# Sigmoid attention with a mixture of experts on one core: the half slots' first layer multiplies the high weights with high and low tokens in one product

## The chip, the core and the metric

The kernel runs on one core of a Trainium2 chip. TensorE (PE) multiplies matrices and leaves the sums in eight banks of PSUM, each 128 partitions by 512 fp32 columns. VectorE (DVE), ScalarE (ACT) and GpSimd (POOL) do the rest, each one instruction at a time in the order of the program. SyncE (SP) starts most DMAs. The metric is device time of one execution in microseconds.

## The reference

Attention runs on 8 batches of 12 heads, 448 tokens and 64 dimensions, with a sigmoid in place of the softmax. Its output, seen as 3584 tokens of 768 numbers, goes through 8 experts, of which each token uses one:

```
attn = 1 / (1 + exp(-(scale * q @ k.T - log(S))));  x = (attn @ v) as 3584 x 768
e_idx = argmax(x @ w_gate, 1)
gate_w = softmax(x @ w_gate)[e_idx];  eom = sigmoid(x @ w_output_gate)
for e in range(8):
    h = maximum(x[e_idx == e] @ w1[e], 0)          # 768 -> 1024
    out[e_idx == e] = gate_w * eom[:, e] * (h @ w2[e])   # 1024 -> 768
```

All data are fp32.

## The kernel before

The first half of the span computes attention and the lists of tokens of each expert. Then come the experts, in slots of one expert each. A full slot takes TB = 448 tokens, a half slot TM = 240. In the profiled execution seven full slots and two half slots run (the diff touches the half slots alone); up to six more half slots stand in the program and are skipped by a branch.

Every fp32 operand is split into a high part, rounded to a format that TensorE takes at full rate, and a low part, the remainder. A product is the sum of three: high by high, high by low, low by high. ACT makes the high part (L414, a cast) and DVE the low part (L415, a subtraction).

**Layer 1 of a half slot** makes eight blocks f = 0 to 7 of 128 hidden features. A block sums over six pieces d of the 768 inputs, three products each: wh·xh (L467), wh·xl (L468), wl·xh (L469), each 240 columns, all into one PSUM bank. Three banks (`psh`) rotate, so block f + 3 may start only when the last reader of block f is done. The readers are the relu on ACT (L496, writes the high part hh) and one DVE instruction (L497, max(ps, 0) − hh, the low part hl). In the loop over f (L589), behind blocks 1 to 4, `split_w2(f - 1)` splits two rows of the second layer's weights: two casts on ACT, two subtractions of 768 columns on DVE. Behind blocks 2 to 4 SP is given the next slot's w1 loads (L400), which overwrite the raw w2 rows just split.

**Layer 1 of a full slot** already joins wh·xh and wh·xl: `xs` lies as 448 high and 448 low columns side by side, so products of 512, 384 and 448 columns do it, and the 64 columns that lie in the wrong place are copied to SBUF and added back by DVE (`join`, L485 and L486) ahead of the relu.

**Layer 2 of a half slot** has four pieces of 24 products of 384 columns (L527 to L529), each evicted on ACT (L534). Around them ACT and DVE split the next slot's w1 and tokens.

**Pending blocks.** A full slot leaves the last two of its six output blocks in PSUM. The next slot's `finish` (L539) turns them: per block `join`, then a DVE transpose (L517), then eight DMAs to DRAM, four loads back, scaling on ACT (L564) and scatters on POOL. `slot` calls `next(fin)` for the turning at L587, ahead of layer 1, in both kinds of slot.

The instructions of each engine stand in the order in which the program gives them (`manual_schedule`). Between the full slots and the first half slot lies the end of nested branches (L932), where each engine also waits for its own DMAs.

Of the kernel before, what the change touches and what calls it, by code (L numbers as in the profile page):

```python
# [8 lines left out]
F32 = mybir.dt.float32  # L9
# [4 lines left out]
ALU = mybir.AluOpType  # L14
# [8 lines left out]
DM = H * D  # L23
DF = 1024
# [4 lines left out]
Q4 = DM // 4  # L29
G = 2  # L30
TB = 448
TM = 240
GB_, GM = TB // 32, -(-TM // 32)
# [19 lines left out]
def r32(ap):  # L53
    return ap.bitcast(F32)


class Kernel:
# [19 lines left out]
    def memory(self):  # L77
        self.rounded = self.pool("rounded").tile([128, ROUNDED // 4], F32R, name="rounded")
        self.plain = self.pool("plain").tile([128, PLAIN // 4], F32, name="plain")
        ps = self.pool("psum", space=PSUM).tile([128, 8, 512], F32, name="ps")  # L80
        self.ps_s = [ps[:, 0:2], ps[:, 2:4]]
        self.ps_o = [[ps[:, 4], ps[:, 5]], [ps[:, 6], ps[:, 7]]]
        self.ps_s2 = ps[:, 6:8]
        self.psh = [ps[:, i] for i in (0, 1, 2)]
        self.psy = [ps[:, i] for i in (4, 5, 3)]
        self.ps_step = ps[:, 3, 0:8]
        self.rot = {}
        self.beat = [None, None]
        self.hints = {2: [ET.Activation, ET.DVE, ET.Pool]}

        c = self.carve
        w = c(0, 3, 2, 2, DF)
        self.w1s = [[w[:, d // 2, a, d % 2] for d in range(6)] for a in range(2)]
        self.w1p = [[w[:, k, a] for k in range(3)] for a in range(2)]
        self.x2 = c(12 * DF * 4, 6, 2 * TB)
        self.xs = [self.x2[:, :, TB * i:TB * i + TB] for i in range(2)]
        self.slots_begun = 0

        self.w1r = c(0, 6, DF, dt=F32)
        self.w2r = c(0, 8, DM, dt=F32)  # L100
        self.xg = c(6 * DF * 4, GB_, Q4, dt=F32)
        self.xT = c(6 * DF * 4 + XG, 6, TB, dt=F32)
        self.yq = c(6 * DF * 4 + XG, GB_, Q4, dt=F32)
        self.xTm = c(6 * DF * 4 + XG, 6, 32 * GM, dt=F32)
        self.spare = c(6 * DF * 4 + GM * Q4 * 4, DM, dt=F32), c(6 * DF * 4 + XG + 6 * 32 * GM * 4, DM, dt=F32)

    def late_memory(self):
# [350 lines left out]
    def layer1_mm(self, f, n):  # L458
        nc = self.nc
        ps = self.h_ps = self.take("h", self.psh)  # L460
        c = slice(128 * f, 128 * f + 128)
        (wh, wl), (xh, xl) = self.w1s, self.xs
        for d in range(6):
            if n == TB and self.joined:
                mm = self.products(ps, wh[d][:, c], wl[d][:, c], self.x2[:, d], d == 0, d == 5)
            else:
                nc.tensor.matmul(ps[:, 0:n], wh[d][:, c], xh[:, d, 0:n], start=(d == 0), stop=False)  # L467
                nc.tensor.matmul(ps[:, 0:n], wh[d][:, c], xl[:, d, 0:n], start=False, stop=False)  # L468
                mm = nc.tensor.matmul(ps[:, 0:n], wl[d][:, c], xh[:, d, 0:n], start=False, stop=(d == 5))  # L469
            if d == 2:  # L470
                self.beat[1] = mm.ins
# [16 lines left out]
    def layer1(self, f, n, begun=False):  # L488
        nc = self.nc
        if not begun:  # L490
            self.layer1_mm(f, n)
        if n == TB and self.joined:
            self.join(self.h_ps)
        ps = self.h_ps[:, 0:n]
        hh, hl = (h[:, f, 0:n] for h in self.hs)
        self.beat[0] = nc.scalar.activation(hh, ps, AF.Relu).ins  # L496
        nc.vector.scalar_tensor_tensor(hl, ps, 0.0, r32(hh), ALU.max, ALU.subtract)  # L497

# [80 lines left out]
    def slot(self, cur, nxt, side=None, begun=False, hint=None):  # L579
        nx = None  # L580
        if nxt is not None:
            nx, rows, sure = nxt() if callable(nxt) else nxt
            last = -(-nx["lx"].shape[1] // 2) - 1
        n = 32 * cur["lx"].shape[1]
        lag = 0 if self.left is not None or n == TB else 2
        fin = self.finish(n)
        next(fin, None)  # L587
        self.rot["y"] = 1
        for f in range(8):  # L589
            if begun and f == 1:  # L590
                self.change_step()
            self.layer1(f, TB if n == TB else TM, begun and f == 0)
            if nx is not None and n < TB:
                if f >= lag:
                    self.gather_rows(nx, f - lag, rows, 1)
                if f == 7 and lag == 0:
                    self.nc.gpsimd.drain()
            elif nx is not None and f <= last:
                self.gather_rows(nx, 2 * f, rows, 1)
                self.gather_rows(nx, 2 * f + 1, rows, 0)  # L600
                if f == last and not sure:
                    self.nc.gpsimd.drain()
            if f == 6 and n < TB:
                next(fin, None)
            if side is not None:
                next(side, None)
            if 1 <= f < 5:
                self.split_w2(f - 1)
                if f > 1:
                    self.load_w1(nx, f - 2)  # L610
        if lag == 0:
            for k in range(3):
                self.turn_x(nx, k)
        if n == TB:
            next(fin, None)
            self.layer2_columns(cur, nx, side, hint, fin)
            self.slots_begun += 1
            return nx
        ws = {0: (0, 1), 1: (2,)}
        for i in range(4):  # L620
            t = i // 2
            self.layer2(cur, t, i % 2, self.ys[t])
            if nx is not None:
                if lag and i == 0:
                    for g in range(8 - lag, 8):
                        self.gather_rows(nx, g, rows, g % 2)
                    self.nc.gpsimd.drain()  # L627
                for k in ws.get(i, ()):
                    self.split_w1(k)
                    for j in range(k, 4 if k == 2 else k + 1):  # L630
                        self.load_w2(nx, j)
                if lag and i == 0:
                    for k in range(3):
                        self.turn_x(nx, k)
                if i < 3:
                    self.split_x(nx, i)
            if i < 2:
                next(fin, None)
            if side is not None:
                next(side, None)  # L640
            if hint is not None and i == 1:
                self.tc.mark_branch_hint_location(hint, hint="LikelyTaken", engines=[ET.SP])
        return nx
# [342 lines left out]
```

## Time and profile before

| what | value |
|---|---|
| three runs, median | 750.63 us (749.03 to 752.99) |
| profiled execution | 749.12 us, its span 747.3 us |
| PE busy | 739.1 us, 99% of the span |
| DVE, ACT, POOL busy | 447.2, 369.8, 250.4 us |
| first half slot, layer 1 | 674.93 to 691.13 us |
| second half slot, layer 1 | 707.78 to 723.91 us |

A timeline row gives the start and the duration in us, the engine, the line, the operation with what it writes and reads, and in brackets how long the engine was idle before it and what ended that. Products on PE overlap: a row's duration is longer than the distance from one start to the next, and the distance is what one product costs. The names `plain` and `rounded` are two large buffers in which many smaller ones are carved out.

### The profile page before, as it was taken

How to read it: one execution, taken by the hardware profiler on the slowest of the kernel's cores; microseconds unless marked ns; L12 is line 12 of the kernel's file. 1: busy time of each engine (PE TensorE's matmuls, PEld its weight loads, DVE VectorE, ACT ScalarE, POOL GpSimd, SP SyncE). 2: the span in 40 equal slices, each digit the busy share in tenths (PEclk: the TensorE clock that was granted, in tenths of full speed). 3: DMA queues.
4: the chain of work that ended last, by engine and by line, in shares of the span. 5: the costliest groups of instructions: out<-in, count | busy, mean ns of one | idle time of the engine just before them, and what ended most of it. 6: DMA issues, size and time to landing. Idle time of an engine off the chain costs nothing. (4 is left out here: it accounts for less than half of the span.)

```text
span 747.3 us, 14681 instructions
## 1 busy us (share of the span) xinstructions
PE 739.1 (99%) x5576; PEld 544.7 (73%) x5576; DVE 447.2 (60%) x895; ACT 369.8 (49%) x437; POOL 250.4 (34%) x375
## 2 busy tenths in 40 slices
PE   9999999999999999999999999999999999999996
PEld 4334444444344469999999999999999999999996
DVE  1333863585777849916746746646655655656555
ACT  5666676566777734404514514514514423434644
POOL 5000130022254435246525315325224234234351
PEclk9999999999999999999999999999999999999999
DMA  8464656647495755366386386386386485576951
GB/s 283 149 206 144 193 140 195 188 122 212 172 331 184 208 135 180 132 167 199 113 297 216 131 265 221 118 277 205 147 274 183 177 272 174 188 227 202 328 200 46
DMA packets 90647, 145.76 MB, mean 195 GB/s; under 512 B 16738, under 2 KB 67298, under 8 KB 90560
## 3 DMA queue, kind: packets, MB, share of 16 engines
q1 hardware_dynamic: 79808, 119.22, 51.6%
q0 software_dynamic: 9680, 24.53, 9.3%
q10 hardware_dynamic: 1072, 0.92, 0.5%
q8 instruction: 46, 0.75, 0.4%
q14 instruction: 41, 0.34, 0.1%
HBM read 118.40 MB, written 32.62 MB: 202 GB/s over the span
## 5 line engine op out<-in xcount | busy, mean ns | idle before, releaser
L718 ACT ACTIVATE a<-ps,small 128x896 f32<-128x896 f32 x168 | 168.6, 1007 | 85.6 <-PE ps L716 83.3
L716 PE MATMUL ps<-q,k 64*64 64x448 f32 x1344 | 157.6, 542 | 0.0
L389 POOL DMA_INDIRECT plain<-x_dram,lxs x112 | 111.0, 991 | 134.1 <-ACT h L496 63.4
L725 PE MATMUL ps<-a,v 64*64 64x448 f32 x1344 | 155.9, 536 | 0.0
L496 ACT ACTIVATE h<-ps 128x448 fp32r<-128x448 f32 (+1 forms) x72 | 36.4, 506 | 204.8 <-DVE ps L486 132.2
L479 PE MATMUL ps<-rounded 128*128 128x512 f32 x288 | 112.0, 389 | 0.0
L479 PE MATMUL ps<-h,w2h 128*128 128x512 f32 x288 | 112.0, 389 | 0.0
L716 PEld LDWEIGHTS ps<-q,k 64*64 64x64 f32 x1344 | 50.5, 134 | 76.5 <-issue 69.8
L725 PEld LDWEIGHTS ps<-a,v 64*64 64x64 f32 x1344 | 51.0, 133 | 75.4 <-issue 71.4
L481 PE MATMUL ps<-rounded 128*128 128x448 f32 x288 | 105.1, 365 | 0.0
L481 PE MATMUL ps<-h,w2l 128*128 128x448 f32 x288 | 105.1, 365 | 0.0
L415 DVE TENSOR_TENSOR rounded<-plain,rounded 128x2048 fp32r<-128x2048 f32 (+5 forms) x63 | 96.4, 1566 | 10.8 <-ACT rounded L414 10.8
L480 PE MATMUL ps<-rounded 128*128 128x384 f32 x288 | 95.9, 333 | 0.0
L480 PE MATMUL ps<-h,w2h 128*128 128x384 f32 x288 | 95.9, 333 | 0.0
L414 ACT CAST rounded<-plain 128x2048 fp32r<-128x2048 f32 (+5 forms) x63 | 82.0, 1332 | 24.0 <-DVE plain L434 22.8
L571 POOL DMA_INDIRECT out<-y,lts x24 | 42.9, 1786 | 106.3 <-ACT y L564 103.3
L485 DVE COPY hb<-ps 128x64 f32<-128x64 f32 x84 | 18.5, 220 | 94.8 <-PE ps L481 76.6
L415 DVE TENSOR_TENSOR w2l<-plain,w2h 128x768 fp32r<-128x768 f32 x72 | 65.7, 954 | 4.4 <-ACT w2h L414 1.9
L497 DVE SCALAR_TENSOR_TENSOR h<-ps,h 128x448 fp32r<-128x448 f32 (+1 forms) x72 | 41.1, 574 | 40.0 <-ACT h L496 35.1
L481 PEld LDWEIGHTS ps<-rounded 128*128 128x128 f32 x288 | 54.1, 188 | 11.1
L481 PEld LDWEIGHTS ps<-h,w2l 128*128 128x128 f32 x288 | 54.1, 188 | 11.1
L254 POOL TENSOR_TENSOR meta<-eom,den 64x1 f32<-64x1 f32 (+1 forms) x40 | 8.0, 199 | 152.2 <-DVE eom L251 150.5
(170 smaller groups left out, 1058.7 us busy)
## 6 DMA issues: line engine op xcount, KB each, us to landing
plain<-w SPq DMA_DIRECT2D x40, 768.0 KB
plain<-w SPq DMA_DIRECT2D x27, 1024.0 KB
k<-kT SPq DMA_DIRECT2D x23, 448.0 KB
q<-qT SPq DMA_DIRECT2D x23, 448.0 KB
x_dram<-xt SPq DMA_DIRECT2D x30, 336.0 KB
v<-vm SPq DMA_DIRECT2D x23, 384.0 KB
y<-y_dram SPq DMA_DIRECT2D x18, 384.0 KB
y_dram<-plain SPq DMA_DIRECT2D x28, 192.0 KB
```

The lines of the kernel that those rows point to most:

```text
L389: self.paced(self.nc.gpsimd.indirect_dma_start(out=self.xg[:, g], out_offset=None, in_=x4, in_offset=bass.IndirectOffsetOnAxis(ap=s["lx"][ ...
L414: self.nc.scalar.copy(hi, raw)
L415: self.nc.vector.tensor_tensor(lo, raw, r32(hi), ALU.subtract)
L479: mm(ps, wh, both[:, 0:512], start=first, stop=False)
L480: mm(ps[:, 512 - TB:TB], wh, both[:, 512:2 * TB], start=False, stop=False)
L481: return mm(ps[:, 0:TB], wl, both[:, 0:TB], start=False, stop=last)
L496: self.beat[0] = nc.scalar.activation(hh, ps, AF.Relu).ins
L497: nc.vector.scalar_tensor_tensor(hl, ps, 0.0, r32(hh), ALU.max, ALU.subtract)
L571: i = self.nc.gpsimd.indirect_dma_start(out=self.out, out_offset=bass.IndirectOffsetOnAxis(ap=at, axis=0), in_=y, in_offset=None, bounds_c ...
L716: qk = nc.tensor.matmul(ps[half[h], j, 0:S], k[half[j], e, o:o + 64], q[half[j], e], start=True, stop=True)
L718: self.beat[0] = nc.scalar.activation(at[u % 3], ps[:, :, 0:S], AF.Sigmoid, bias=self.bias_s, scale=1.0 / math.sqrt(D)).ins
L725: nc.tensor.matmul(self.ps_o[e][h][half[j], 0:S], v[half[h], e, c, j], a[half[h], j], start=(i in ((0, 3 if h else 4)[e],)), stop=(i == (2 ...
```

## The change

For half slots the products wh·xh and wh·xl become one product of 480 columns: high tokens give columns 0 to 239, low tokens columns 240 to 479 of the bank. wl·xh is added to columns 0 to 239 as before. ACT then copies columns 240 to 479 to a new SBUF buffer `rest_m`, and DVE adds them onto columns 0 to 239, ahead of the relu. In half slots the turning of the pending blocks moves from ahead of block 0 to behind it. `rest_m` lies in `plain`, in a place that holds other data in full slots. Full slots are unchanged.

```
+        self.rest_m = c(6 * DF * 4 + (GM * Q4 + DM) * 4, TM, dt=F32)
...
         for d in range(6):
-            if n == TB and self.joined:
+            if n == TM:
+                both = self.x2[:, d].rearrange("p (a t) -> p a t", a=2)[:, :, 0:n]
+                nc.tensor.matmul(ps[:, 0:2 * n].rearrange("p (a t) -> p a t", a=2), wh[d][:, c], both,
+                                 start=(d == 0), stop=False)
+                mm = nc.tensor.matmul(ps[:, 0:n], wl[d][:, c], xh[:, d, 0:n], start=False, stop=(d == 5))
+            elif self.joined:
                 mm = self.products(ps, wh[d][:, c], wl[d][:, c], self.x2[:, d], d == 0, d == 5)
...
-        if n == TB and self.joined:
-            self.join(self.h_ps)
         ps = self.h_ps[:, 0:n]
         hh, hl = (h[:, f, 0:n] for h in self.hs)
+        if n == TM:
+            nc.scalar.copy(self.rest_m, self.h_ps[:, TM:2 * TM])
+            nc.vector.tensor_tensor(ps, ps, self.rest_m, ALU.add)
+        elif self.joined:
+            self.join(self.h_ps)
         self.beat[0] = nc.scalar.activation(hh, ps, AF.Relu).ins
...
         fin = self.finish(n)
-        next(fin, None)
+        if n == TB:
+            next(fin, None)
...
             self.layer1(f, TB if n == TB else TM, begun and f == 0)
+            if f == 0 and n < TB:
+                next(fin, None)
```

In the changed kernel the copy is L501, the add L502, the relu L505, the low part L506, the cast L415, the subtraction L416, the join L491 and L492, the transpose L526.

On DVE, at the start of the first half slot, stood before (w2l is the low part of w2, h the hidden features, hb the buffer of the join):

```order
L485 COPY hb<-ps 128x64
L486 TENSOR_TENSOR ps<-ps,hb 128x64
L517 STREAM_TRANSPOSE plain<-ps 128x14x32
L485 COPY hb<-ps 128x64
L486 TENSOR_TENSOR ps<-ps,hb 128x64
L517 STREAM_TRANSPOSE plain<-ps 128x14x32
L497 SCALAR_TENSOR_TENSOR h<-ps,h 128x240 x2
L415 TENSOR_TENSOR w2l_2640<-plain,w2h_2638 128x4x6x32 x2
L497 SCALAR_TENSOR_TENSOR h<-ps,h 128x240
L415 TENSOR_TENSOR w2l_2640<-plain,w2h_2638 128x4x6x32 x2
```

The same place in the changed kernel:

```order
L502 TENSOR_TENSOR ps<-ps,plain 128x240
L506 SCALAR_TENSOR_TENSOR h<-ps,h 128x240
L491 COPY hb<-ps 128x64
L492 TENSOR_TENSOR ps<-ps,hb 128x64
L526 STREAM_TRANSPOSE plain<-ps 128x14x32
L491 COPY hb<-ps 128x64
L492 TENSOR_TENSOR ps<-ps,hb 128x64
L526 STREAM_TRANSPOSE plain<-ps 128x14x32
L502 TENSOR_TENSOR ps<-ps,plain 128x240
L506 SCALAR_TENSOR_TENSOR h<-ps,h 128x240
L416 TENSOR_TENSOR w2l_2640<-plain,w2h_2638 128x4x6x32 x2
L502 TENSOR_TENSOR ps<-ps,plain 128x240
```

The two turnings now stand between block 0 and block 1, and an add stands ahead of every low part, behind the two subtractions of the block before.

On ACT, at the same place, stood before (w2h is the high part of w2):

```order
L496 ACTIVATE h<-ps 128x240 x2
L414 CAST w2h_2638<-plain 128x4x6x32 x2
L496 ACTIVATE h<-ps 128x240
L414 CAST w2h_2638<-plain 128x4x6x32 x2
L496 ACTIVATE h<-ps 128x240
```

The same place in the changed kernel:

```order
L501 COPY plain<-ps 128x240
L505 ACTIVATE h<-ps 128x240
L501 COPY plain<-ps 128x240
L505 ACTIVATE h<-ps 128x240
L415 CAST w2h_2638<-plain 128x4x6x32 x2
L501 COPY plain<-ps 128x240
L505 ACTIVATE h<-ps 128x240
```

Each relu now stands behind a copy on its own engine, and between the two lies the add on DVE; the casts of `split_w2` stay behind the relu.

## Rows read from the trace of the kernel before

**Rows 1.** The page, part 1: busy time, share and instructions of each engine.

```profile
PE 739.1 (99%) x5576; PEld 544.7 (73%) x5576; DVE 447.2 (60%) x895; ACT 369.8 (49%) x437; POOL 250.4 (34%) x375
```

**Rows 2.** Stretches: length, busy of PE, PEld, DVE, ACT, POOL, granted clock, DMA.

```profile
674.00:691.09 17.09, 16.53 (x146) 16.22 (x146) 11.59 (x21) 8.30 (x15) 8.89 (x8) 1.00 0.63 185
740.50:747.30 6.80, 0.22 (x2) 0.00 (x0) 1.90 (x3) 0.58 (x1) 0.96 (x1) 0.75 0.18 53
```

**Rows 3.** Timeline, PE: first products of both layers in both half slots.

```profile
674.93 0.35 PE L467 MATMUL ps<-rounded 128*128 128x240 f32 x1 [0.56 <-DVE hb L485]
...
691.13 0.34 PE L527 MATMUL ps<-w2h,h 128*128 128x384 f32 x1
...
707.78 0.27 PE L467 MATMUL ps<-rounded 128*128 128x240 f32 x1
...
723.91 0.34 PE L527 MATMUL ps<-w2h,h 128*128 128x384 f32 x1
```

**Rows 4.** Timeline, PE: four products of a full slot's layer 1.

```profile
628.01 0.39 PE L479 MATMUL ps<-rounded 128*128 128x512 f32 x1
628.24 0.33 PE L480 MATMUL ps<-rounded 128*128 128x384 f32 x1
628.41 0.36 PE L481 MATMUL ps<-rounded 128*128 128x448 f32 x1
628.61 0.39 PE L479 MATMUL ps<-rounded 128*128 128x512 f32 x1
```

**Rows 5.** Timeline, DVE: one block of a full slot's layer 1.

```profile
631.26 0.22 DVE L485 COPY hb<-ps 128x64 f32<-128x64 f32 x1
631.51 0.23 DVE L486 TENSOR_TENSOR ps<-ps,hb 128x64 f32<-128x64 f32 x1
632.42 0.62 DVE L497 SCALAR_TENSOR_TENSOR h<-ps,h 128x448 fp32r<-128x448 f32 x1 [0.68 <-ACT h L496]
633.14 1.83 DVE L415 TENSOR_TENSOR w2l<-plain,w2h 128x768 fp32r<-128x768 f32 x2
634.88 0.22 DVE L485 COPY hb<-ps 128x64 f32<-128x64 f32 x1
```

**Rows 6.** Timeline, ACT: the same block.

```profile
631.84 0.55 ACT L496 ACTIVATE h<-ps 128x448 fp32r<-128x448 f32 x1 [1.62 <-DVE ps L486]
632.28 1.55 ACT L414 CAST w2h<-plain 128x768 fp32r<-128x768 f32 x2
```

**Rows 7.** Timeline, ACT: first half slot, layer 1.

```profile
677.27 0.37 ACT L496 ACTIVATE h<-ps 128x240 fp32r<-128x240 f32 x1 [8.64 <-PE ps L469]
...
682.09 0.37 ACT L496 ACTIVATE h<-ps 128x240 fp32r<-128x240 f32 x1 [0.90 <-ACT w2h L414]
682.36 1.56 ACT L414 CAST w2h<-plain 128x768 fp32r<-128x768 f32 x2
```

**Rows 8.** Timeline, DVE: first half slot, turning and layer 1.

```profile
678.16 0.65 DVE L517 STREAM_TRANSPOSE plain<-ps 128x448 f32<-128x448 f32 x1 [3.16 <-SPq L932]
...
679.79 0.68 DVE L497 SCALAR_TENSOR_TENSOR h<-ps,h 128x240 fp32r<-128x240 f32 x2
...
683.22 1.83 DVE L415 TENSOR_TENSOR w2l<-plain,w2h 128x768 fp32r<-128x768 f32 x2 [0.31 <-ACT w2h L414]
684.96 0.40 DVE L497 SCALAR_TENSOR_TENSOR h<-ps,h 128x240 fp32r<-128x240 f32 x1
```

**Rows 9.** Line 932, POOL's queue: count, least/median/most ns, first and last start.

```profile
L932 POOLq INC_SWDGE_SEM  x1: 280/280/280, 676.9 to 676.9; - x1
```

**Rows 10.** Timeline, SP, ACT and DVE: first half slot, next slot's weights and tokens.

```profile
685.38 4.17 SPq L400 DMA_DIRECT2D plain<-w  x3
...
695.63 0.58 ACT L534 ACTIVATE y<-ps,ltb 128x384 f32<-128x384 f32 x1 [3.86 <-PE ps L529]
...
708.37 0.69 DVE L415 TENSOR_TENSOR rounded<-plain,rounded 128x512 fp32r<-128x512 f32 x1 [0.23 <-ACT rounded L414]
```

**Rows 11.** Timeline, ACT: second half slot, last casts of w2.

```profile
720.25 1.57 ACT L414 CAST w2h<-plain 128x768 fp32r<-128x768 f32 x2 [1.42 <-DMA plain<-w]
```

## The prediction, as it was put on record

> **What bounds the kernel now.** I read the page's busy shares first: PE is busy 99% of the span, the others at most 60% [rows 1]. So whatever shortens PE's stream shortens the kernel, and whatever makes PE wait lengthens it. The stretch table then shows the first half slot's layer 1 with PE at 16.53 of 17.09 us, the missing 0.56 us being the pause at the end of the nested branches, and granted clock 1.00, the level of 2.4 GHz [rows 2]. PE's timeline gives the block: 144 products of 240 columns from 674.93 to 691.13, 112.5 ns each, 2.02 us per block; the second half slot needs 16.13 us for the same, so PE never waits there [rows 3]. Last I read DVE and ACT, since they hold the PSUM banks that PE needs back. They are nearly full in the blocks with weight splits: DVE's two subtractions take 1.74 us (683.22 to 684.96) and the low part 0.3 to 0.4 beside PE's 2.02 [rows 8].
>
> **What PE gains.** Each d loses one product and gets a wider one. In a full slot 512, 384 and 448 columns cost 0.23, 0.17 and 0.20 us from start to start [rows 4], so 480 columns, halfway between 448 and 512, cost 0.215. Before: 3 x 0.1125 = 0.3375 per d. After: 0.215 + 0.1125 = 0.3275. That is 0.01 x 48 = 0.5 us per half slot, 1.0 us in all, and a block of 1.96 us. No row shows moving columns taken from two pieces. The bounds are the two measured widths around it: at 0.20 the gain is 0.025 x 96 = 2.4 us, at 0.23 it is a loss of 0.005 x 96 = 0.5. I take the middle between them.
>
> The Trainium skill, "TensorE: Matmul & The Clock Gate", section "Back-to-back issue gap", gives a warm product columns / 2.4 GHz plus about 2.5 ns: 102.5 ns for 240 columns. The rows have 112.5, so by it a dropped product saves 2.5 ns, 0.24 us over 96, in place of 1.0. The measurement decides, and the forecast below hardly uses either.
>
> **What the change adds on ACT and DVE.** Per block a copy of 240 columns out of PSUM on ACT (priced as the relu of that width, 0.37 us [rows 7]) and an add of 240 columns on DVE. The add with 64 columns starts 0.33 us ahead of the relu that waits for it (631.51 to 631.84) [rows 5, 6]. The low part costs 0.62 us at 448 columns and 0.40 at 240 [rows 5, 8], so 176 more columns are about 0.19, and add to relu is 0.52 us. Bounds for it: 0.33 (width free) and 0.95 + 0.1 (a subtraction of 768 columns).
>
> Alone these are small. What matters is that they tie two queues into a ring. Before, ACT's relu and DVE's low part waited for PE and each other's last result only, and the casts ran ahead of the subtractions. Now block f + 1's relu waits for its add, the add stands in DVE's queue behind the two subtractions of block f, these wait for the casts, and the casts stand in ACT's queue behind block f's relu. One turn of the ring: add to relu 0.52; relu to cast 0.27 (682.09 to 682.36); first cast to first subtraction 0.86 (682.36 to 683.22); the two subtractions to the next instruction 1.74 (683.22 to 684.96) [rows 7, 8]. Sum 3.39 us, against PE's 1.96. The full slots already run this ring: 631.26 to 634.88 is 3.62 us, and its parts, 0.25 + 0.33 + 0.44 + 0.86 + 1.74, make 3.62 [rows 5, 6]. There it hides since a block takes PE 3.6 us (6 x 0.60 [rows 4]); a half slot's block takes half of that.
>
> **First half slot.** Block 0 leaves PE at 674.93 + 1.96 = 676.89. Before, the relu came 0.32 behind the block's end (677.27 against 676.95); so the copy starts at 677.21. The copy waits newly for POOL's queues, whose counter is set at 676.9 + 0.28 = 677.18 [rows 9]: just in time, and I add 0.04. Behind ACT stand only the relu and casts, which wait anyway. Copy end and handover 0.41: add at 677.66, relu 678.18, low part 678.59, DVE free at 678.90. Now come the two turnings: the first join 0.51, then 1.63 as before from the first transpose to the low part (678.16 to 679.79) [rows 8], so add 1 starts at 681.04. The 3.16 us that DVE waited for SP ahead of its first transpose is covered now by block 0 [rows 8], which gains little: that wait ran beside PE's block 0. Behind the moved turnings SP's eight DMAs to DRAM start some 1.2 us later.
>
> Adds 2, 3, 4 follow every 3.39: 684.43, 687.82, 691.21. A low part ends 0.52 + 0.41 + 0.40 = 1.33 behind its add's start, and PE may go on about 0.15 later. Block 7 needs the bank of block 4: 691.21 + 1.33 + 0.15 = 692.69. It ends at 694.65, where layer 2 began at 691.13: **3.5 us later**. PE should stand before blocks 5, 6 and 7 for 1.2, 1.4 and 1.4 us, less the 0.5 it gains. Blocks 5 to 7 are not followed by splits; their ring is 1.6 us and layer 2, which reads h in the order of f, meets them in time.
>
> What follows shifts with PE rather than more: ACT's casts of the next slot's w1 stand behind the first eviction of layer 2 (695.63) [rows 10]. One detail: the next slot's last token split ended at 708.37 + 0.69 = 709.06, and the merged product of d = 4 reads the low tokens 0.15 us sooner than L468 did; 0.1 us.
>
> **Second half slot**, from its start, with no pending blocks: block 1 ends at 3.92, add 1 at 3.92 + 0.32 + 0.41 = 4.65, add 4 at 4.65 + 3 x 3.39 = 14.82, block 7 may start at 14.82 + 1.48 = 16.30 and ends at 18.26 instead of 16.13: **2.1 us later**. Here PE waits before blocks 6 and 7 alone. The weights' arrival doesn't set it: the last casts waited for a DMA at 720.25, 12.5 us in [rows 11], and in the ring they come at 15.6. The tail behind PE stays.
>
> **Sum.** 3.5 + 0.1 + 2.1 = 5.7 us. The profiled execution took 749.1 us (747.3 of span and 1.8 around it), so 754.8; the median of the three runs is 1.5 higher and would give 756.3. I predict 755.5.
>
> **Rivals.**
> - *Three banks hide it* (not slower). If the ring turned in 2.0 us in the first half slot and 2.5 in the second, block 7 would find its bank free, and only PE's gain of 1.0 would be left: 748.1 by the profile, 749.6 by the median. For it: at PE's own pace block 4's low part would be done 1.7 us ahead of block 7 in the second half slot (13.72 - 4.65 - 5.88 - 1.48). Against it: three turns that are 1.4 us too slow use 4.3, and three parts of the ring are rows of this very stretch. It decides from a turn of 2.5 us downward; with an add at its lower bound the turn is still 3.2.
> - *The next slot's weights come late* (more). w1 loads went out from 685.38 on [rows 10], behind the subtractions that free their place; in the ring the last subtraction ends about 694.6 instead of 689.1, 5.5 us later where PE loses 3.5. If the last load or the loads of the pending rows behind it then bind, the second half slot starts up to 2 us later still: 757.5. Against it: ACT has two casts of 2048 columns ahead of the third load's.
> - *PE's clock falls* (more). The rows show 1.00 through the pause of 0.56 us, and 0.75 only in the last stretch, when PE has finished [rows 2, 3]. Pauses of 1.4 us are not in the rows. If a block after each of the five pauses ran at the lower level, 1.2 GHz, it would cost 2 us each time: 765. The same page of the Trainium skill advises, in "Why this matters for your kernels", against pauses between bursts of products, as the clock halves behind long ones; the trace shows none long enough to try it, and such a fall is this rival.
> - *The ring is shorter than I make it*, by a quarter (casts or subtractions that overlap more): 2.6 us a turn leaves 1.2 in the first half slot and nothing in the second, 750 to 751.5.
>
> **How the numbers follow.** Forecast 0.68, hidden 0.09, shorter ring 0.10, late weights 0.09, clock 0.04. With the forecast's own error of 1.5 us (add between its bounds moves a turn by -0.2 to +0.5, six turns, -1.1 to +3.2) its range is 753.5 to 758.5. The range 750.5 to 759.5 leaves out the hidden case and the clock, and the ends of the others. A measurement of this kernel tells 0.5%, 3.75 us, from no change: slower begins at 754.4 against the median. The hidden and short cases and the lower part of the forecast are "same"; nothing but a gain of PE four times as large would be faster. Faster 0.02, same 0.25, slower 0.73.
>
> **What would show it.** Right: in blocks 1 to 4 of both half slots DVE's adds (L502) stand some 3.4 us apart, relus wait for adds, PE waits for L506 before blocks 6 and 7, and layer 2 begins 3.5 and then 2.1 us later in its slot. Wrong: adds 2 us apart, or PE without a gap in layer 1; or a gap at the second half slot's start, which would be the late weights; or a granted clock under 1.00 in the half slots. The steps that would fail are the ring's 3.39 us and the slack of three banks.

## The result, and the profile after

The changed kernel takes 755.21 us (median of 6 runs, 753.77 to 755.87) against 749.64 us (6 runs, 747.79 to 752.99). The ratio, which is that of the means (754.97 and 749.95), is 1.0067, 95% interval 1.0043 to 1.0091: slower by 0.4 to 0.9%. The forecast was 755.5. The profiled execution took 755.87 us, its span 754.1.

The stretch table of the changed kernel, cut at the starts of the two half slots' layers (length, busy of PE, PEld, DVE, ACT, POOL, granted clock, DMA), first both layers 1 and then the end:

```profile
675.15:694.57 19.42, 16.58 (x97) 14.41 (x97) 13.05 (x25) 9.46 (x19) 8.15 (x8) 1.00 0.62 185
711.23:729.61 18.38, 16.66 (x98) 14.34 (x97) 12.45 (x22) 10.74 (x22) 11.85 (x11) 1.00 0.67 248
...
746.50:754.10 7.60, 0.00 (x0) 0.00 (x0) 1.49 (x3) 0.56 (x1) 1.48 (x1) 0.76 0.16 46
```

Layer 1 takes 19.42 us where it took 16.20, and 18.38 where it took 16.13 [rows 3]: 3.22 + 2.25 = 5.5 us. The products are fewer, the time is longer, and PE has idle time inside. These are PE's pauses, from its timeline, with the first product of layer 2 between the two slots:

```profile
675.15 0.45 PE L467 MATMUL ps<-rounded 128*128 128x480 f32 x1 [0.56 <-PEq L944]
685.87 0.48 PE L467 MATMUL ps<-rounded 128*128 128x480 f32 x1 [0.68 <-DVE h L506]
689.18 0.49 PE L467 MATMUL ps<-rounded 128*128 128x480 f32 x1 [1.09 <-DVE h L506]
692.49 0.49 PE L467 MATMUL ps<-rounded 128*128 128x480 f32 x1 [1.07 <-DVE h L506]
694.57 0.34 PE L536 MATMUL ps<-w2h,h 128*128 128x384 f32 x1
...
724.22 0.49 PE L467 MATMUL ps<-rounded 128*128 128x480 f32 x1 [0.58 <-DVE h L506]
727.53 0.49 PE L467 MATMUL ps<-rounded 128*128 128x480 f32 x1 [1.08 <-DVE h L506]
```

Each is the first product of a block (5, 6, 7, then 6, 7), and each waits for L506, the low part of the block three before, which still holds its PSUM bank. What makes L506 late is read on DVE and ACT. DVE, first half slot:

```profile
677.78 0.42 DVE L502 TENSOR_TENSOR ps<-ps,plain 128x240 f32<-128x240 f32 x1 [11.57 <-ACT plain L501]
678.63 0.41 DVE L506 SCALAR_TENSOR_TENSOR h<-ps,h 128x240 fp32r<-128x240 f32 x1 [0.44 <-ACT h L505]
...
679.61 0.65 DVE L526 STREAM_TRANSPOSE plain<-ps 128x448 f32<-128x448 f32 x1 [0.17 <-DVE ps L492]
...
681.24 0.38 DVE L502 TENSOR_TENSOR ps<-ps,plain 128x240 f32<-128x240 f32 x1
682.06 0.41 DVE L506 SCALAR_TENSOR_TENSOR h<-ps,h 128x240 fp32r<-128x240 f32 x1 [0.44 <-ACT h L505]
682.82 1.83 DVE L416 TENSOR_TENSOR w2l<-plain,w2h 128x768 fp32r<-128x768 f32 x2 [0.35 <-ACT w2h L415]
684.56 0.41 DVE L502 TENSOR_TENSOR ps<-ps,plain 128x240 f32<-128x240 f32 x1
685.41 0.41 DVE L506 SCALAR_TENSOR_TENSOR h<-ps,h 128x240 fp32r<-128x240 f32 x1 [0.44 <-issue]
686.13 1.83 DVE L416 TENSOR_TENSOR w2l<-plain,w2h 128x768 fp32r<-128x768 f32 x2 [0.31 <-ACT w2h L415]
687.88 0.41 DVE L502 TENSOR_TENSOR ps<-ps,plain 128x240 f32<-128x240 f32 x1
```

ACT beside it:

```profile
683.43 0.35 ACT L501 COPY plain<-ps 128x240 f32<-128x240 f32 x1
685.01 0.37 ACT L505 ACTIVATE h<-ps 128x240 fp32r<-128x240 f32 x1 [1.23 <-DVE w2l L416]
685.27 1.56 ACT L415 CAST w2h<-plain 128x768 fp32r<-128x768 f32 x2
```

One turn of the ring can be followed through the times of the last two fences: add 684.56, relu 685.01, first cast 685.27, first subtraction 686.13, next add 687.88, so 3.32 us. The copy at 683.43 is done long before the add that uses it. In the turn DVE stands idle twice (0.44 and 0.31) and ACT once (1.23), while PE waits: no engine is full, and the order holds all three, which e4 and e9 below put to the test. Before, DVE's longest idle stretch in the blocks with splits was 0.31 us [rows 8] and PE never waited.

### The profile page after: what moved, and what is told of

The parts are those of the page before. It is cut to its first block, busy times and chain, and to the rows that moved or that the text cites. A ratio compares the mean times of both kernels' runs of the same rounds, so it can differ in the third digit from the quotient of the medians.

```text
span 754.1 us, 14509 instructions
## 1 busy us (share of the span) xinstructions
PE 740.2 (98%) x5480; PEld 553.6 (73%) x5480; DVE 453.8 (60%) x911; ACT 374.8 (50%) x453; POOL 253.1 (34%) x375
## 5 line engine op out<-in xcount | busy, mean ns | idle before, releaser
L728 PE MATMUL ps<-q,k 64*64 64x448 f32 x1344 | 163.2, 541 | 0.0
L737 PE MATMUL ps<-a,v 64*64 64x448 f32 x1344 | 161.6, 536 | 0.0
L505 ACT ACTIVATE h<-ps 128x448 fp32r<-128x448 f32 (+1 forms) x72 | 36.4, 506 | 201.1 <-DVE ps L492 124.5
L728 PEld LDWEIGHTS ps<-q,k 64*64 64x64 f32 x1344 | 57.6, 134 | 70.3 <-issue 62.1
L737 PEld LDWEIGHTS ps<-a,v 64*64 64x64 f32 x1344 | 58.2, 133 | 69.2 <-issue 63.5
L416 DVE TENSOR_TENSOR rounded<-plain,rounded 128x2048 fp32r<-128x2048 f32 (+5 forms) x63 | 96.4, 1566 | 8.5 <-ACT rounded L415 8.5
L415 ACT CAST rounded<-plain 128x2048 fp32r<-128x2048 f32 (+5 forms) x63 | 82.0, 1333 | 24.5 <-DVE plain L435 23.2
L491 DVE COPY hb<-ps 128x64 f32<-128x64 f32 x84 | 18.5, 220 | 85.8 <-PE ps L487 78.0
L416 DVE TENSOR_TENSOR w2l<-plain,w2h 128x768 fp32r<-128x768 f32 x72 | 65.8, 955 | 5.0 <-ACT w2h L415 1.9
L506 DVE SCALAR_TENSOR_TENSOR h<-ps,h 128x448 fp32r<-128x448 f32 (+1 forms) x72 | 41.4, 575 | 40.6 <-ACT h L505 38.6
```

Source lines behind the costliest of these rows:

```text
L415: self.nc.scalar.copy(hi, raw)
L416: self.nc.vector.tensor_tensor(lo, raw, r32(hi), ALU.subtract)
L728: qk = nc.tensor.matmul(ps[half[h], j, 0:S], k[half[j], e, o:o + 64], q[half[j], e], start=True, stop=True)
L737: nc.tensor.matmul(self.ps_o[e][h][half[j], 0:S], v[half[h], e, c, j], a[half[h], j], start=(i in ((0, 3 if h else 4)[e],)), stop=(i == (2 ...
```

## The experiments

The ratios are to the kernel before, run beside each group on the same chip; there it took 748.30 us (19 runs) for e1 to e4, 748.42 (27) for e5 to e7 and 748.49 (21) for e8 and e9. The times expected for e1 to e7 are on the scale of 749.6, so they are compared as differences to before. The changed kernel itself was not run again beside them; its own difference is 5.57 us between the medians.

**Without the splits, changed kernel (e1) and kernel before (e2).** Both:

```
-                self.split_w2(f - 1)
+                if n == TB:
+                    self.split_w2(f - 1)
```

> The changed kernel without split_w2 in half slots, so their second layer multiplies with split weights left from an earlier expert. Ring theory: with no casts and subtractions in it a turn takes about 1.2 us (the adds of blocks 5, 6 and 7 stand 1.17 us apart in the changed kernel), less than a block's 1.96, so PE has no gap in layer 1, which takes about 15.7 us in both half slots: about 748.7 us, 6.5 less than the changed kernel. Rival (the wide product, or the bare hand-over from ACT to DVE and back, holds PE): the gaps ahead of blocks 5 to 7 stay, at least 753 us.

> The kernel before, likewise without split_w2 in half slots. Ring theory: PE waited for neither, so the time is that of before, 749.6 us within 1. Less the time of the run above it gives what the wide product alone is worth: about 1.0 us (0.01 us in each of 96 pieces d). Rival (the splits already cost time before): 747 or less.

e1: 750.25 us, ratio 1.0028 (1.0018 to 1.0038), 1.95 over before, where the theory had 0.9 under it and the rival at least 3.4 over it: neither held as a whole. e2: 748.39, ratio 1.0003 (0.9993 to 1.0012), as expected. The stretches of both layers 1 in e1 show where the theory held:

```profile
673.86:689.62 15.76, 15.76 (x97) 14.40 (x97) 7.57 (x20) 5.02 (x14) 7.26 (x8) 1.00 0.56 154
706.28:724.53 18.25, 16.16 (x98) 14.33 (x97) 9.23 (x17) 8.53 (x20) 9.90 (x10) 1.00 0.70 252
```

The first is 15.76 us, without a pause: with the splits gone nothing holds PE, and the wide product is as quick as forecast. (This takes work away from ACT and DVE as well as the ring; e9 below separates the two.) But the second slot lost 2.1 us at its start, at the third product pair, ahead of tokens or weights that were not yet split (PE's timeline):

```profile
709.19 0.46 PE L467 MATMUL ps<-rounded 128*128 128x480 f32 x1 [2.09 <-DVE rounded L416]
```

ACT, which casts them, had waited in the layer 2 ahead, once before two casts of w1 (`issue`: for nothing that the profile shows) and once for the pending rows that SP loads back:

```profile
697.83 2.43 ACT L415 CAST rounded<-plain 128x2048 fp32r<-128x2048 f32 x2 [1.40 <-issue]
701.92 1.86 ACT L573 ACTIVATE plain<-plain,left 128x768 f32<-128x768 f32 x2 [1.66 <-DMA plain<-y_dram]
```

So a second limit lies right behind the first. I took it for the moved turnings: SP's eight DMAs to DRAM stand ahead of the w1 loads and of the pending rows' loads in its queue, and they now start behind block 0's add and low part. SP's timeline in e1:

```profile
680.06 5.17 SPq L562 DMA_DIRECT2D y_dram<-plain  x8
685.62 2.37 SPq L401 DMA_DIRECT2D plain<-w  x3
```

In e2 they start at 677.76. In the profile of before they start at 679.89, but PE's layer 1 began later there too: counted from its first product, the eight DMAs start at 4.96 us before, without a loss, and at 6.20 in e1. Of the three w1 loads the first goes out later in e1 (11.76 us behind that product against 10.45) and the last sooner (by 14.1 against 14.6), so the moment of issue alone doesn't explain the wait.

**Five PSUM banks (e3).**

```
+        self.psh_m = [ps[:, i] for i in (0, 1, 2, 6, 7)]
...
-        ps = self.h_ps = self.take("h", self.psh)
+        ps = self.h_ps = self.take("m", self.psh_m) if n == TM else self.take("h", self.psh)
```

> The changed kernel with five PSUM banks in place of three for layer 1 of half slots (banks 6 and 7 are free there). Ring theory: PE no longer waits in layer 1, but the ring goes on at 3.3 us a turn, the low part of block 7 is done no sooner, and the gaps move into the first piece of layer 2, ahead of blocks 5 to 7 of the features: about 755.0 us, within 0.7 of the changed kernel. Rival (three banks are the bottleneck, two more blocks of slack cover the ring): about 749 us.

754.68 us, ratio 1.0089 (1.0073 to 1.0106): no gain, and 6.4 over before, 1 us more than expected. The pauses left layer 1 and came back in layer 2, where h of blocks 5, 6 and 7 is read (PE; the line numbers are one higher in this kernel):

```profile
694.33 0.45 PE L537 MATMUL ps<-w2h,h 128*128 128x384 f32 x1 [1.68 <-ACT h L506]
695.50 0.44 PE L537 MATMUL ps<-w2h,h 128*128 128x384 f32 x1 [0.28 <-ACT h L506]
696.66 0.44 PE L537 MATMUL ps<-w2h,h 128*128 128x384 f32 x1 [0.28 <-ACT h L506]
```

The first half slot's layer 1 takes 15.75 us here and its layer 2 20.04 instead of 16.7. The banks are where the wait shows, not its cause: this ring is too slow in every turn, and two more buffers only put the wait off.

**Turned ahead of block 0 (e4).**

```
-        if n == TB:
-            next(fin, None)
+        next(fin, None)
...
-            if f == 0 and n < TB:
-                next(fin, None)
```

> The changed kernel with the pending blocks turned ahead of block 0, as before. Ring theory: DVE waits for SP until about 678.2 ahead of the first transpose, turns until 680.0, and the first two blocks follow: add 1 at about 681.2 as in the changed kernel, so 755.2 us within 0.7. Rival (the moved turnings cost the first half slot their 2.1 us): about 753 us.

753.60 us, ratio 1.0069 (1.0052 to 1.0086), against 1.0067 for the changed kernel: with the ring closed the place of the turnings makes no difference that these times can tell. The trace is not as even. Its two layers 1 are 1.09 and 0.48 us shorter than the changed kernel's:

```profile
675.08:693.41 18.33, 16.30 (x96) 14.40 (x97) 12.65 (x24) 9.36 (x19) 8.03 (x8) 1.00 0.65 196
710.08:727.98 17.90, 16.23 (x97) 14.33 (x97) 11.43 (x20) 10.02 (x20) 9.38 (x9) 1.00 0.61 237
```

In this execution SP let the first transpose go at 677.27 and not at the 678.2 that I had counted on, so add 1 came 4.98 us behind PE's start and not 6.1. It is one profile of each kernel, and whether the move costs the closed ring something is open.

**Only the move (e7)**, in the kernel before.

```
+            if f == 0 and n < TB:
+                next(fin, None)
```

> The kernel before, with only the turnings moved behind block 0. Ring theory: relu, low part and subtractions wait for PE alone, DVE repeats every 2.1 us, the turnings stand 0.3 us later than before: 749.6 us within 0.7. Rival (the move is what costs the first half slot): 751 to 753 us.

748.51 us, ratio 1.0004 (0.9996 to 1.0013). The loss is not the move's by itself; the eight DMAs start 5.48 us behind PE's first product here, and the second layer 1 takes 16.16 us.

**The ring opened (e5), and spread wider (e6).** A half slot's block now reads, for e5, with the w1 loads given out behind blocks 2, 4 and 5 instead of 2, 3 and 4:

```
CASTS = ((), (0, 1), (2, 3), (4, 5), (6, 7), (), (), ())
SUBS  = ((), (0,), (1, 2), (3, 4), (5, 6), (7,), (), ())
...
        nc.scalar.copy(self.rest_m, self.h_ps[:, TM:2 * TM])
        for r in casts[0:1]:
            self.cast_row(r)
        nc.vector.tensor_tensor(ps, ps, self.rest_m, ALU.add)
        for r in subs[0:1]:
            self.rest_row(r)
        ... relu on ACT, low part on DVE as before ...
        for r in casts[1:]:
            self.cast_row(r)
        for r in subs[1:]:
            self.rest_row(r)
```

> The changed kernel with the ring opened: in blocks 1 to 4 the first cast stands between copy and relu on ACT, and each subtraction waits for a cast made half a block earlier; one subtraction stands between add and low part, one behind it. No work is left out. Ring theory: a turn is then DVE's own work, 0.31 + 0.31 + 2 x 0.87 = 2.4 us instead of 3.3. In the first half slot, where the turnings make add 1 late, PE still waits about 0.5 us each ahead of blocks 6 and 7, in the second nowhere: 16.6 and 15.7 us of layer 1, about 749.6 us, 5.5 less than the changed kernel. Rival (DVE's and ACT's amount of work sets it, not the order): about 755 us.

> As the run above, and the eight subtractions spread over blocks 1 to 6 instead of 1 to 5, one beside each of the first three, with the next slot's w1 loads given out behind blocks 3, 5 and 6. Ring theory: DVE has 1.5 us of work in blocks 2 and 3 and at most 2.4 later, PE finds every bank free, layer 1 takes 15.7 us in both half slots: about 748.7 us, 0.9 less than before, and the w1 loads, up to 3 us later than before, still come ahead of ACT's casts. Rival (the w1 loads bind): a gap at the second half slot's start, 750 to 751 us.

e5: 750.93 us, ratio 1.0028 (1.0017 to 1.0039), 2.5 over before, where the theory had before's own time and the rival the changed kernel's: with the same work on every engine, the order gives back about half of the loss. Of the 2.5 us its profile shows 0.5 in the layers 1 (16.36 and 16.44 us, 32.80 against 32.33) and 0.9 in a longer tail behind PE; in the second, PE loses 0.76 us against e8's free layer below, 0.49 of it in the first block. The rest of the 2.5 is not placed. e6: 751.31, ratio 1.0039 (1.0027 to 1.0051), 2.9 over before, where the theory had 0.9 under it and the rival 0.4 to 1.4 over it. The rival's gap is there, larger than it said, as PE's one pause in the second layer 1:

```profile
710.85 0.45 PE L501 MATMUL ps<-rounded 128*128 128x480 f32 x1 [2.84 <-DVE rounded L419]
```

There the w1 loads bind: in the layer 2 ahead ACT waited 1.35 and 2.62 us for them.

**Turned ahead again, without splits (e8) and with the ring opened (e9).** The edit of e4, on e1 and on e5.

> The changed kernel without split_w2 in half slots (their second layer multiplies with split weights left from an earlier expert) and with the pending blocks turned ahead of block 0. Theory of the late DMAs: without splits and with the turnings moved, PE lost 2.1 us at the second half slot's start, since the eight DMAs to DRAM, and with them the w1 loads behind them on SP, went out some 2 us later; turned ahead they go out as before, ACT's casts no longer wait for DMAs, and that gap is gone: both layers 1 in 15.7 to 15.9 us, about 748.2 us, 2 less than with the turnings moved and 0.1 to 0.7 under before. Rival (the second half slot's tokens and weights can't be split any sooner once layer 1 is shorter, whenever the DMAs go out): the gap stays, about 750 us.

> The opened ring (first cast between copy and relu, subtractions half a block behind their casts, all work done) with the pending blocks turned ahead of block 0. Theory of the late DMAs: the w1 loads go out some 1.3 us earlier than in the opened ring with the turnings moved, and the 0.6 us that PE lost there at the second half slot's start goes: layer 1 of about 16.3 and 15.7 us, about 750.2 us, 0.6 less than the opened ring, and 1 to 2 over before, since DVE starts its work of layer 1 late. Rival (the DMAs are no matter there): 751 us, as the opened ring.

The times expected here are on a scale of about 748.5. e8: 748.30 us, ratio 0.9998 (0.9989 to 1.0007), as expected. SP's DMAs go out at 677.76 and 683.50, 2.3 and 2.1 us sooner than in e1, and both layers 1 run free:

```profile
677.76 5.35 SPq L562 DMA_DIRECT2D y_dram<-plain  x8
683.50 2.37 SPq L401 DMA_DIRECT2D plain<-w  x3
```

```profile
674.00:689.76 15.76, 15.76 (x96) 14.40 (x97) 7.27 (x19) 5.00 (x14) 7.25 (x8) 1.00 0.67 207
706.43:722.11 15.68, 15.68 (x97) 14.32 (x97) 6.06 (x15) 5.69 (x15) 8.25 (x9) 1.00 0.72 277
```

What the earlier start buys stands in the DMA share (last but one) of four microseconds, first in e1, then in e8:

```profile
678.00:682.00 4.00, 4.00 (x27) 3.63 (x26) 2.89 (x9) 1.35 (x4) 2.06 (x3) 1.00 0.35 102
678.00:682.00 4.00, 4.00 (x27) 3.66 (x26) 1.99 (x6) 1.72 (x5) 2.58 (x4) 1.00 0.78 228
```

From 682 to 698 us the DMA engines are full in both (0.97 and 0.98). The likeliest reading is that ACT waits for their backlog, which ends sooner when it begins sooner; no run shows that by itself. In e8 neither of e1's two waits on ACT is left.

e9, which leaves nothing out: 748.96 us, ratio 1.0006 (0.9997 to 1.0015), better than expected and no longer to be told from before. It does e4's work on every engine with the turnings in the same place, and differs from it in the order of the splits and in when the w1 loads are given out: the order alone is worth 1.0069 against 1.0006. DVE is nearly full (13.09 of 15.75 us in the first layer 1) and PE free:

```profile
674.82:690.57 15.75, 15.75 (x96) 14.39 (x97) 13.09 (x26) 9.93 (x22) 8.29 (x8) 1.00 0.64 186
707.24:723.10 15.86, 15.86 (x97) 14.32 (x97) 11.91 (x22) 10.72 (x23) 9.38 (x10) 1.00 0.72 277
```

```profile
683.87 0.41 DVE L452 TENSOR_TENSOR ps<-ps,plain 128x240 f32<-128x240 f32 x1
684.19 0.95 DVE L442 TENSOR_TENSOR w2l<-plain,w2h 128x768 fp32r<-128x768 f32 x1
685.06 0.39 DVE L456 SCALAR_TENSOR_TENSOR h<-ps,h 128x240 fp32r<-128x240 f32 x1
685.38 0.94 DVE L442 TENSOR_TENSOR w2l<-plain,w2h 128x768 fp32r<-128x768 f32 x1
686.25 0.40 DVE L452 TENSOR_TENSOR ps<-ps,plain 128x240 f32<-128x240 f32 x1
```

A turn is 2.38 us (683.87 to 686.25), as worked out, without idle time. In this run SP let DVE's first transpose go at 676.57, in the run of before at 678.16 [rows 8]; that gave DVE a start which I hadn't counted on, and I expected 16.3 us where 15.75 came. No version beats the kernel before by more than these runs can tell. PE gains 0.72 us in e9 (31.61 against 32.33 in both layers 1), and the most that the wide product has to give is e8's 0.89.

## Why the prediction was right, point by point

- *PE's gain.* Forecast 0.5 us per half slot; 16.20 - 15.76 = 0.44 and 16.13 - 15.68 = 0.45 where nothing holds PE (e8).
- *The ring's turn.* Forecast 3.39 us, measured 3.32: the relu starts 0.45 us behind the add's start instead of 0.52. From the low part's end to PE I had put 0.15 us without a row; it is 0.05 (685.41 + 0.41 to 685.87).
- *Add 1 of the first half slot.* Forecast 6.11 us behind PE's start (681.04 from 674.93), measured 6.09 (681.24 from 675.15), turnings and POOL's counter included.
- *Layer 2's start.* Forecast 3.5 and 2.1 us later in its slot, measured 3.22 and 2.25. In the first the shorter turns and the hand-over make the difference. In the second, PE waited before blocks 6 and 7 and block 7 started at 16.30 us, both as forecast, but by errors that cancel: the first block lost 0.48 us, for which I had put 0.1, since the last splits of weights and tokens came just too late, and the shorter turns and the hand-over gave 0.4 back. PE's third and fifth pair and block 1, and among them the last split on DVE:

```profile
711.99 0.45 PE L467 MATMUL ps<-rounded 128*128 128x480 f32 x1
712.10 0.69 DVE L416 TENSOR_TENSOR rounded<-plain,rounded 128x512 fp32r<-128x512 f32 x1 [0.26 <-ACT rounded L415]
712.94 0.45 PE L467 MATMUL ps<-rounded 128*128 128x480 f32 x1
713.67 0.38 PE L467 MATMUL ps<-rounded 128*128 128x480 f32 x1
```

- *The sum.* 5.7 forecast; 5.57 between the medians, 5.0 between the means, 6.75 between the two profiled executions (755.87 and 749.12), of which the layers 1 are 5.47. That the total came within 0.2 is in part luck; what held is the mechanism and, to 0.3 us, both slots' terms. That the ring is the cause is shown by e4, e8 and e9, with the turnings in one place: 1.0069 with the splits in the ring, 0.9998 without them, 1.0006 with the same splits out of the ring.
- *The rivals.* "Three banks hide it" fell with the pauses, and e3 showed that five don't either. The shorter ring fell with 3.32. The granted clock stayed at 1.00, the level of 2.4 GHz, through all pauses, e6's 2.84 us among them (its stretches are below); so the fall of the clock found no case here. "The next slot's weights come late" didn't decide the changed kernel, where it had the 0.48 us above, but it is the next limit: it cost 2 us and more as soon as the ring was out of the way with the turnings still moved (e1, e6).

Stretches of e6 around its pause (granted clock third from the end):

```profile
707.18:711.00 3.82, 0.98 (x6) 0.68 (x6) 2.93 (x3) 3.82 (x7) 2.14 (x2) 1.00 0.98 355
711.00:715.00 4.00, 3.95 (x23) 3.39 (x24) 1.48 (x3) 1.39 (x4) 2.15 (x2) 1.00 0.97 326
```

Two terms were wrong without being seen in the sum. I priced the eight DMAs behind the moved turnings at nothing, since PE was late anyway. That cover is the ring itself: take it away and the move costs 2 us (e1 against e8, and likewise e5 against e9). And "the tail behind PE stays" did not hold: about 1 us of the profiled span's 6.8 lies behind PE's end (6.9 us of tail before, 8.0 after, counted from the last product's start); the two layers 1 and a start 0.2 us later make the rest.

## What to carry to other kernels

An instruction that makes two in-order queues wait for each other in turn is not priced by its own duration. Write out one turn of the ring it closes, queue order included, and set that against the pace of the engine it feeds; a stage that already runs the same ring, here the full slots, gives the sum for nothing. When a ring is too slow in every turn, more buffers only move the wait (e3), and putting independent work between its two halves takes it away (e9). Then look at what the slack was covering: here the DMAs behind a moved step.

## What was not expected of the hardware

The last scatter on POOL took 1.48 or 1.49 us in each profiled run with the wide product, and 0.96 in each of the three runs without it (before, e2, e7), although POOL's instructions stand in the same order. POOL, the changed kernel, and then the kernel before:

```profile
747.34 1.48 POOL L580 DMA_INDIRECT out<-y,ltb  x1 [3.15 <-ACT y L543]
```

```profile
741.68 0.96 POOL L571 DMA_INDIRECT out<-y,ltb  x1 [3.17 <-ACT y L534]
```

It is half a microsecond at the very end of the span, it would take back most of PE's gain in e9, and its cause stays open: no run here was made for it.
